# Attention and mixture-of-experts kernel: the loads of the last batch's first pair of heads move in front of the second block's first kept stores

## The chip, the cores and the metric

The kernel runs on 1 core of one Trainium2 chip. Its time is the device time of one execution in microseconds (us), and the number that counts is the median over runs. TensorE is called PE here (PEld is its weight load), VectorE is DVE, ScalarE is ACT, GpSimd is POOL and SyncE is SP. SP does no arithmetic: it issues nearly all loads and stores, one after the other, in the order in which they stand in its queue.

## The reference

The kernel computes two layers one after the other. The first is a linear attention over 4 batches, 8 heads, 576 positions and 64 features a head, with 128 random features; the second is a mixture of 4 experts over all 2304 rows, where every expert is applied to every row and the results are weighted.

```python
def phi(x):                                   # x: (4, 8, 576, 64), omega: (128, 64)
    h = einsum('bhsd,md->bhsm', x, omega) - sum(x * x, -1) / 2
    return exp(h - max(h, -1)) / sqrt(128)
q_p, k_p = phi(q * scale), phi(k * scale)
kv, z = einsum('bhsm,bhsd->bhmd', k_p, v), sum(k_p, axis=2)
x = einsum('bhsm,bhmd->bhsd', q_p, kv) / (einsum('bhsm,bhm->bhs', q_p, z) + 1e-6)
x = x.transpose(0, 2, 1, 3).reshape(2304, 512)
p = probs / (probs.sum(-1) + 1e-9)            # (2304, 4)
out = sum over e of p[:, e] * (maximum(x @ w1[e], 0) @ w2[e])   # w1: (4, 512, 1024), w2: (4, 1024, 512)
```

## The kernel before

**Tiling.** Heads are worked on in pairs, 4 pairs a batch. The 2304 rows of the second layer are cut into blocks: rows 0 to 511 (block 0), rows 512 to 1279 (block 1, 6 tiles of 128) and rows 1280 to 2303 (block 2, 8 tiles). The hidden layer is cut into 8 pieces (expert and half of its 1024 columns), and one piece on one block is a *visit*. Block 1 has 8 visits and block 2 has 8. Each fp32 product is made of three products of rounded halves, so each weight matrix is split into a high part (`w1ah`, `w1sh`, `w2h`, by ACT) and a low part (`w1al`, `w1sl`, `w2l`, by POOL, line 567).

**A visit of block 1** (`fast`). The first matrix product is done in seven partial products with summed operands (`p1` to `p7`, line 934) for each of two groups, and gives the hidden tiles `hh` (ACT, lines 958 and 992) and `hl` (DVE, lines 964 and 995). The second product (`outputs`, lines 753 to 755) runs over six row tiles; three of them are begun early between the partial products. After the last partial product PE needs `hh` and `hl` of line 992 and 995 for the fourth weight chunk of the first row tile. Results are gathered into `acc`.

**Kept weights.** The summed and split first weights that a visit of block 1 makes are stored to memory for block 2: `keep_sides`, line 670, 8 stores a visit, named `kept`. They stand on SP's queue. The next visit's weights go to the same two buffers: the split into `w1ah` (line 564, called as the first step of `sides(v + 1)`) rewrites a buffer which the first store, `kept<-w1ah`, still reads, so it waits until that store has landed. It stands on ACT's queue after `p6(1)`, in front of the three `hh` of `p7(1)`, `p3(1)` and `p4(1)`:

```python
        p3(0)
        if u == 1:
            keep_sides(v)
        p4(0)
        ...
        p6(1)
        if v + 1 != DEEP[0]:
            next(ready, None)      # the split into w1ah
        begun(0)
        p7(1)
```

**The order of the work around it** is written out by hand. The attention of the last batch (4 pairs, `Halves`) is cut into steps, *ticks*, that are run between the pieces of block 1: `opening` is 6 ticks for the first pair (load k, load q, load v and the tails, square k, square q, sum of squares of k), `later_ticks` is 12 ticks a pair and ends with 48. `emit` lets 54 ticks run in the first 80% of the block. A visit has 7 shares: one after the partial products and one after each row tile. Loads go through `Halves.load` (line 247: kd, kn, qd, qn), `load_v` (line 128) and `load_tails` (lines 132 and 133). Between them, SP also issues the raw weights `w1r` and `w2r` (line 549). Every load on SP goes round eight semaphores, and an issue also waits for the landing of the issue eight before it.

Of the kernel before, what the change touches and what calls it, by code (L numbers as in the profile page):

```python
# [14 lines left out]
def attention_moe(ctx, tc, kT, qT, kd, qd, kn, qn, vn, omT, probs, w1, w2, out):  # L15
# [11 lines left out]
    _, NP, D, _ = kT.shape  # L27
# [3 lines left out]
    E, FP, P, _ = w1.shape  # L31
# [18 lines left out]
    def place(hp):  # L50
        return hp % 2 * 2 + hp // 2
# [17 lines left out]
    def f32(ap):  # L69
        return ap.bitcast(F32)  # L70
# [30 lines left out]
    NV = len(HALVES)  # L101
# [136 lines left out]
    class Halves(Pair):  # L238
# [131 lines left out]
        def times(self, part):  # L370
            nu, dn, n = self.num.pop(part)
            for o, c, m in in_ring(self.b * S + 2 * P * part, n):
                nc.gpsimd.tensor_tensor(raw_x[:, place(self.hp), c:c + m], nu[:, o:o + m], dn[:, o:o + m], ALU.mult)

    def opening(p, both=False):

        p.load("k")
        yield
        p.load("q")
        yield  # L380
        p.load_v()
        p.load_tails()
        yield
        p.square("k")
        yield
        p.square("q")
        yield
        p.lengths("k")
        if both:
            p.lengths("q")  # L390
        yield
# [74 lines left out]
    def later_ticks(pairs):  # L466

        for p, then in zip(pairs, pairs[1:] + [None]):
            p.project("k")
            p.project_tails("k")  # L470
            p.maxima("k")
            p.maxima_tails("k")
            p.bias("k")
            yield
            p.exp_tails("k")
            p.exp("k", 0)
            p.lengths("q")
            yield
            p.exp("k", 1)
            yield  # L480
            p.project("q")
            p.project_tails("q")
            p.maxima("q")
            p.maxima_tails("q")
            p.bias("q")
            yield
            p.exp_tails("q")
            p.exp("q", 0)
            if then:
                then.load("k")  # L490
            yield
            p.exp("q", 1)
            if then:
                then.load("q")
            yield
            p.sum_keys()
            if then:
                then.load_v()
                then.square("k")
            yield  # L500
            p.turn(0)
            yield
            p.turn(1)
            if then:
                then.square("q")
            yield
            p.numerators(0)
            if then:
                then.lengths("k")
            yield  # L510
            p.invert(0)
            p.times(0)
            p.numerators(1)
            yield
            p.invert(1)
            p.times(1)
            yield
# [4 lines left out]
    BIG = {1: (START, 6 * P), 2: (START + 6 * P, 8 * P)}  # L522
# [5 lines left out]
    N0 = len(visits)  # L528
# [134 lines left out]
    def keep_sides(v):  # L663

        for i in range(2):
            kept[visits[v][1:3], i] = ts_ = tuple(
                scratch.tile([P, w * H], F32, tag=f"s{visits[v][1:3]}{i}{x}{w}", name="kept", bufs=1) for w in (3, 4) for x in "hl"
            )
            for k, t in zip(ts_, made.pop((v, i))):
                nc.sync.dma_start(k, f32(t))  # L670
# [127 lines left out]
    def store(keep):  # L798
        while len(stores) > keep:
            i, t = stores.pop(0)  # L800
            nc.sync.dma_start(out[i * P:(i + 1) * P], t)
# [90 lines left out]
    def fast(v):  # L892
# [96 lines left out]
        def p4(g):  # L989
            product(g, 4, "u", start=False)  # L990
            ha, hc = (x[:, :n] for x in hs[2 * g + 1])
            nc.scalar.activation(ha, P_[g]["u"], AF.Relu)
            if deep and g == 0:
                nc.scalar.activation(r11[:, 1], P_[0]["u"], AF.Relu)
            nc.vector.scalar_tensor_tensor(hc, P_[g]["u"], 0.0, f32(ha), ALU.max, ALU.subtract)  # L995

        def p3(g):
            product(g, 3, "b5", start=False)
            both(g, 0, 1, "b5", "u2")
# [131 lines left out]
                start_sides2(v + 1)  # L1131
        p3(0)
        if u == 1:
            keep_sides(v)
        p4(0)
        if deep:
# [179 lines left out]
    def first_visit(g1):  # L1316
        hs = [relu(ps, 2 * P) for ps in g1[:2]]
        yield 0.5
        for ps in g1[2:]:
            split_w(lo=nc.vector)  # L1320
            hs.append(relu(ps, 2 * P))
            yield 0.5
        split_w(lo=nc.vector)
        split_w(lo=nc.vector)
        yield 0.5
        for t in range(2):
            ps = bank("g2")
            outputs(0, hs, ps, t, range(FH))
            gather(0, ps, t)
            gathered(0, t)  # L1330
            split_w()
            split_w(lo=nc.vector)
            yield 1

    def first_rest(pairs, then):

        def ahead(hp):
            if hp < NP:
                pairs[hp].project("q", 1)
                pairs[hp].project("q", 2)  # L1340

        def exps(hp):
            if hp < NP:
                pairs[hp].exp("q", 1)
                pairs[hp].exp("q", 2)

        ahead(0)
        pairs[2].square("q1", nc.gpsimd)
        yield
        exps(0)  # L1350
        ahead(1)
        pairs[3].square("q1", nc.gpsimd)
        yield
        for hp, p in enumerate(pairs):
            if hp:
                pairs[hp - 1].finish(1)
            p.turn(1, nc.vector)
            p.turn(2, nc.vector)
            if hp == 0:
                nc.vector.tensor_scalar(om_r, om_r, QS, None, ALU.mult)  # L1360
            if hp:
                next(then, None)
            yield
            exps(hp + 1)
            ahead(hp + 2)
            if hp:
                next(then, None)
            yield
            p.numerators(1)
            yield  # L1370
        pairs[-1].finish(1)
        yield

    def chain(*many):
        for x in many:
            yield from x
# [3 lines left out]
    def emit():  # L1380
        pairs, g1 = begin()
        later = [Halves(b, hp) for b in range(1, B) for hp in range(NP)]
        windows = {
            0: (first_rest(pairs, opening(later[0], both=True)), 15 / 11),
            3: (joint_ticks(later[:-NP]), 76 / 45.4),
            N0: (chain(opening(later[-NP]), later_ticks(later[-NP:])), 54 / (NV * (BIG[1][1] // P + 1) * 0.8)),
        }
        ticks, n, done, per = iter(()), 0, 0.0, 0
        for v in range(len(visits)):
            if v in windows:  # L1390
                for _ in ticks:
                    pass
                ticks, per = windows[v]
                n, done = 0, 0.0
            for share in first_visit(g1) if v == 0 else fast(v) if v >= N0 else plain(v):
                done += share
                while n < done * per:
                    next(ticks, None)
                    n += 1
        store(0)  # L1400
# [61 lines left out]
```

## Time and profile before

| | us |
|---|---|
| median of 3 runs | 885.14 |
| lowest and highest run | 884.5, 887.36 |
| the profiled execution's own time | 884.03 |
| its span, first to last instruction | 882.3 |
| PE busy | 876.0 (99%) |
| DVE busy | 575.6 (65%) |
| POOL busy | 555.9 (63%) |
| ACT busy | 467.9 (53%) |

Durations come from the one profiled execution, whose span is 1.73 us shorter than its own time. A busy PE is not the same as PE at its peak: matmuls overlap, so the distance from one start to the next is what one costs. Block 1 runs from 284.75 us of the span to 566.6 us, and the first visit of it to 317.6 us.

### The profile page before, as it was taken

The numbers are of one execution on the slowest core, as the hardware profiler recorded it, in microseconds if no ns is written. First come the engines' busy times: TensorE is split into PE (matmuls) and PEld (weight loads), VectorE is DVE, ScalarE is ACT, GpSimd is POOL, SyncE is SP. The second block draws the span as 40 slices with busy tenths as digits, with TensorE's granted clock in tenths as the row PEclk, the third lists the DMA queues.
The fourth block names the chain that finished last, engine by engine and source line by source line (L and its number), as shares of the span: only waits on it lengthen the run. The fifth ranks groups of instructions, "written<-read, shape, count | busy, mean of one in ns | idle before, by whom it ended". The sixth has DMA issues, their size and how long they took to land.

```text
span 882.3 us, 14767 instructions
## 1 busy us (share of the span) xinstructions
PE 876.0 (99%) x5484; PEld 787.8 (89%) x5484; DVE 575.6 (65%) x1025; ACT 467.9 (53%) x1039; POOL 555.9 (63%) x494
## 2 busy tenths in 40 slices
PE   9999999999999999999999999999999999999998
PEld 9988888989888998989889899899989898998988
DVE  6765566766667647576766656975748476574847
ACT  6554677676784565546545554544443434444342
POOL 6656455555644554444445346779898887979874
PEclk9999999999999999999999999999999999999999
DMA  7665355444522757536274355645152442425132
GB/s 184 170 225 155 111 162 173 132 138 138 179 67 60 265 163 259 196 132 240 78 275 169 118 215 183 214 154 158 57 179 82 138 163 85 156 60 180 52 117 96
DMA packets 64296, 134.01 MB, mean 152 GB/s; under 512 B 10368, under 2 KB 20800, under 8 KB 64224
## 3 DMA queue, kind: packets, MB, share of 16 engines
q1 hardware_dynamic: 54256, 102.95, 35.8%
q0 software_dynamic: 9360, 29.82, 10.5%
q8 instruction: 43, 0.70, 0.3%
q10 hardware_dynamic: 608, 0.30, 0.1%
q14 instruction: 29, 0.24, 0.1%
HBM read 98.96 MB, written 34.08 MB: 151 GB/s over the span
## 4 chain that ended last, share of the span: by engine, by line
PE 91%; DVE 3%; POOL 2%; DMA 2%; issue 1%; ACT 1%; SPq 0%; POOLq 0%; ACTq 0%; DVEq 0%
PE g L934 28%; PE g L1012 18%; PE g L753 8%; PE g L755 8%; PE g L754 8%; PE g L738 3%; PE g L739 3%; PE g L740 3%; PE kv L317 2%; PE q_ps L266 1%; PE k_ps L266 1%; PE qt_ps L328 1%; DMA kept<-w1ah 1%; PE kv L177 1%; PE nd L358 1%
## 5 line engine op out<-in xcount | busy, mean ns | idle before, releaser
L782 DVE SCALAR_TENSOR_TENSOR acc<-g,pr,acc 128x256 f32<-128x256 f32 (+1 forms) x278 | 140.4, 543 | 41.2 <-PE g L755 25.7
L567 POOL TENSOR_TENSOR w2l<-w2r,w2h 128x512 fp32r<-128x512 f32 x61 | 79.4, 1309 | 77.4 <-ACT w2h L564 65.3
L567 POOL TENSOR_TENSOR w1sl<-w1r,w1sh 128x512 fp32r<-128x512 f32 (+1 forms) x43 | 75.2, 1751 | 65.2 <-ACT w1sh L564 54.5
L753 PE MATMUL g<-w2h,hh 128*128 128x512 f32 x280 | 112.0, 400 | 0.3 <-ACT kp L299 0.2
L755 PE MATMUL g<-w2h,hl 128*128 128x512 f32 x280 | 109.7, 392 | 0.0
L754 PE MATMUL g<-w2l,hh 128*128 128x512 f32 x280 | 109.5, 391 | 0.0
L934 PE MATMUL g<-xbh,w1sh 128*128 128x384 f32 (+1 forms) x256 | 93.0, 363 | 0.0
L934 PE MATMUL g<-xbl,w1sh 128*128 128x384 f32 (+1 forms) x256 | 92.9, 363 | 0.0
L934 PE MATMUL g<-xbh,w1sl 128*128 128x384 f32 (+1 forms) x256 | 92.6, 362 | 0.0
L940 ACT ACTIVATE sum<-g 128x384 f32<-128x384 f32 (+1 forms) x96 | 52.2, 543 | 69.7 <-PE g L934 68.8
L567 POOL TENSOR_TENSOR w1al<-w1r,w1ah 128x512 fp32r<-128x512 f32 (+1 forms) x45 | 51.5, 1160 | 50.9 <-ACT w1ah L564 32.9
L934 PE MATMUL g<-xbh,w1ah 128*128 128x384 f32 (+1 forms) x192 | 69.9, 364 | 0.0
L934 PE MATMUL g<-xbl,w1ah 128*128 128x384 f32 (+1 forms) x192 | 69.6, 362 | 0.0
L934 PE MATMUL g<-xbh,w1al 128*128 128x384 f32 (+1 forms) x192 | 69.5, 362 | 0.0
L948 DVE TENSOR_TENSOR sum<-g,sum 128x384 f32<-128x384 f32 (+1 forms) x64 | 37.4, 587 | 39.6 <-PE g L934 33.6
L755 PEld LDWEIGHTS g<-w2h,hl 128*128 128x128 f32 x280 | 52.5, 188 | 11.8 <-DVE hl L995 0.4
L753 PEld LDWEIGHTS g<-w2h,hh 128*128 128x128 f32 x280 | 52.7, 188 | 10.9 <-DVE sum L948 0.6
L754 PEld LDWEIGHTS g<-w2l,hh 128*128 128x128 f32 x280 | 52.6, 188 | 9.0
L964 DVE SCALAR_TENSOR_TENSOR hl<-sum,hh 128x384 fp32r<-128x384 f32 x48 | 33.2, 695 | 42.0 <-ACT hh L958 41.3
L934 PEld LDWEIGHTS g<-xbh,w1sh 128*128 128x128 f32 x256 | 48.1, 188 | 5.7 <-DVE sum L948 0.6
L934 PEld LDWEIGHTS g<-xbl,w1sh 128*128 128x128 f32 x256 | 48.1, 188 | 5.2
L934 PEld LDWEIGHTS g<-xbh,w1sl 128*128 128x128 f32 x256 | 48.1, 188 | 5.1
(220 smaller groups left out, 2470.1 us busy)
## 6 DMA issues: line engine op xcount, KB each, us to landing
w1r<-in_w SPq DMA_DIRECT2D x54, 512.0 KB, 3.6
w2r<-in_w SPq DMA_DIRECT2D x76, 256.0 KB, 2.9
kept<-w1sh SPq DMA_DIRECT2D x16, 512.0 KB, 5.0
kept<-w1sl SPq DMA_DIRECT2D x16, 512.0 KB, 5.5
w1sh<-kept POOLq DMA_DIRECT2D x16, 512.0 KB, 5.1
w1sl<-kept POOLq DMA_DIRECT2D x16, 512.0 KB, 5.8
kept<-w1ah SPq DMA_DIRECT2D x16, 384.0 KB, 4.3
kept<-w1al SPq DMA_DIRECT2D x16, 384.0 KB, 4.9
```

Source lines behind the costliest of these rows:

```text
L567: lo.tensor_tensor(c, t, f32(a), ALU.subtract)
L738: nc.tensor.matmul(ps[:, :n], a[:, w], hi, start=(hp == 0), stop=False)
L739: nc.tensor.matmul(ps[:, :n], a[:, w], lo, start=False, stop=False)
L753: nc.tensor.matmul(ps, ha[:, ts_], wa, start=(c == 0), stop=False)
L754: nc.tensor.matmul(ps, ha[:, ts_], wc, start=False, stop=False)
L755: nc.tensor.matmul(ps, hc[:, ts_], wa, start=False, stop=(c == FH - 1))
L782: nc.vector.scalar_tensor_tensor(to, ps, sc, to, ALU.mult, ALU.add)
L934: nc.tensor.matmul(ps, a[:, w], x[:, k], start=(start and k + at == 0), stop=(k == 1 and at == 2), skip_group_check=not start)
L940: nc.scalar.activation(t, P_[g][where], AF.Copy)
L948: nc.vector.tensor_tensor(t, P_[g][where], kept, ALU.add)
L964: nc.vector.scalar_tensor_tensor(x, y, 0.0, f32(z), ALU.max, ALU.subtract)
L1012: nc.tensor.matmul(to, x, w, start=(start and f + k == 0), stop=(f + k == 3), skip_group_check=not start)
```

## The change

The loads of the first pair of the last batch leave the ticks and are issued in `fast`, right before `keep_sides` of block 1's first visit. `opening` keeps three ticks for that pair, and 51 ticks run in the same 80% of the block, so that each of them stands at another place than before, the first ones most.

```diff
+    ahead = []
+
     def opening(p, both=False):
 
-        p.load("k")
-        yield
-        p.load("q")
-        yield
-        p.load_v()
-        p.load_tails()
-        yield
+        if both:
+            p.load("k")
+            yield
+            p.load("q")
+            yield
+            p.load_v()
+            p.load_tails()
+            yield
         p.square("k")
...
         if u == 1:
+            for p in ahead:
+                p.load("k")
+                p.load("q")
+                p.load_v()
+                p.load_tails()
+            ahead.clear()
             keep_sides(v)
...
-            N0: (chain(opening(later[-NP]), later_ticks(later[-NP:])), 54 / (NV * (BIG[1][1] // P + 1) * 0.8)),
+            N0: (chain(opening(later[-NP]), later_ticks(later[-NP:])), 51 / (NV * (BIG[1][1] // P + 1) * 0.8)),
...
+        ahead.append(later[-NP])
```

SP's queue in block 1's first visit, before (k and q are inputs of the pair, va and vb its values, kept the stores, w1r and w2r raw weights):

```order
L549 DMA w2r<-in_w 128x512 x3
L670 DMA kept<-w1ah 128x768
L670 DMA kept<-w1al 128x768
...
L670 DMA kept<-w1sl 128x1024
L549 DMA w2r<-in_w 128x512
L247 DMA k<-in_kd 128x576
...
L133 DMA vb<-in_vn 64x4x64
L549 DMA w1r<-in_w 128x1024 x2
```

The same stretch of SP's queue now (line numbers are three higher behind the diff's first new lines):

```order
L552 DMA w2r<-in_w 128x512 x3
L247 DMA k<-in_kd 128x576
L247 DMA k<-in_kn 128x576
L247 DMA q<-in_qd 128x576
L247 DMA q<-in_qn 128x576
L128 DMA va<-in_vn 128x4x128
L132 DMA vb<-in_vn 64x4x64
L133 DMA vb<-in_vn 64x4x64
L673 DMA kept<-w1ah 128x768
L673 DMA kept<-w1al 128x768
...
L552 DMA w2r<-in_w 128x512
```

Seven loads have moved past eight stores and one weight load; nothing was added to the queue or taken from it.

ACT's queue in the same visit now; before, the same operations stand in the same order, and the first row waits for the same store, under the name of another semaphore:

```order
L567 ACTIVATE w1ah<-w1r 128x512 [waits DMAHW2_49,Pool_49]
L567 ACTIVATE w1ah<-w1r 128x256
L961 ACTIVATE hh<-sum 128x384 [waits DVE_49] x2
L995 ACTIVATE hh<-g_3654 128x384 [waits PE_49]
L783 ACTIVATE acc<-g_3762,pr 128x512 [waits PE_49]
```

The split that waits for the first kept store still stands in front of the last hidden tiles of the visit.

PE's queue, the key projections of the pair (k_ps, t_ps) between the row tiles of the first visit (g_3851 is the fourth tile), before:

```order
L753 MATMUL g_3851<-w2h,hh 128x512
L754 MATMUL g_3851<-w2l,hh 128x512
L755 MATMUL g_3851<-w2h,hl 128x512
L266 MATMUL k_ps<-om_r,k 128x128 x8
L277 MATMUL t_ps<-om_r,k 128x128 x2
L753 MATMUL g_3894<-w2h,hh 128x512
```

And now, where the rows in front of them belong to the second row tile (g_3778):

```order
L756 MATMUL g_3778<-w2h,hh 128x512
L757 MATMUL g_3778<-w2l,hh 128x512
L758 MATMUL g_3778<-w2h,hl 128x512
L266 MATMUL k_ps<-om_r,k 128x128 x8
L277 MATMUL t_ps<-om_r,k 128x128 x2
L756 MATMUL g_3802<-w2h,hh 128x512
```

The projections have moved from behind the fourth row tile to behind the second.

## Rows read from the trace of the kernel before

**Rows 1.** The page, section 1: busy us, share of the span, instructions.

```profile
PE 876.0 (99%) x5484; PEld 787.8 (89%) x5484; DVE 575.6 (65%) x1025; ACT 467.9 (53%) x1039; POOL 555.9 (63%) x494
```

**Rows 2.** Waits of PE, whole span: who waited for whom, us, times, longest.

```profile
PE g L753 <- ACT kp L299: 0.2, 1, 0.2
```

**Rows 3.** Waits of ACT in block 1, same columns.

```profile
ACT w1ah L564 <- DMA kept<-w1ah: 16.8, 9, 3.1
```

**Rows 4.** Timeline of ACT, first visit: start us, us, instruction [idle before, releaser].

```profile
300.33 0.94 ACT L564 ACTIVATE w1ah<-w1r 128x512 fp32r<-128x512 f32 x2 [3.06 <-DMA kept<-w1ah]
...
302.78 0.53 ACT L958 ACTIVATE hh<-sum 128x384 fp32r<-128x384 f32 x1 [1.09 <-DVE sum L948]
303.21 0.47 ACT L992 ACTIVATE hh<-g 128x384 fp32r<-128x384 f32 x1
```

**Rows 5.** Timeline of DVE, same stretch.

```profile
301.71 0.56 DVE L964 SCALAR_TENSOR_TENSOR hl<-sum,hh 128x384 fp32r<-128x384 f32 x1 [2.29 <-ACT hh L958]
...
304.20 0.55 DVE L995 SCALAR_TENSOR_TENSOR hl<-g,hh 128x384 fp32r<-128x384 f32 x1
```

**Rows 6.** Timeline of PE, same stretch.

```profile
304.22 0.39 PE L753 MATMUL g<-w2h,hh 128*128 128x512 f32 x1
304.45 0.39 PE L754 MATMUL g<-w2l,hh 128*128 128x512 f32 x1
304.80 0.50 PE L755 MATMUL g<-w2h,hl 128*128 128x512 f32 x1
```

**Rows 7.** Timeline of SP, first visit of block 1 (issues only).

```profile
296.72 0.42 SPq L670 DMA_DIRECT2D kept<-w1ah  x1
...
304.56 1.13 SPq L549 DMA_DIRECT2D w2r<-in_w  x1
305.79 1.09 SPq L247 DMA_DIRECT2D k<-in_kd  x1
...
309.57 0.60 SPq L133 DMA_DIRECT2D vb<-in_vn  x1
```

**Rows 8.** The store issued at 296.72 alone: issue to landing.

```profile
DMA to landing us min/median/max: 3.5/3.5/3.5
```

**Rows 9.** The weight load issued at 304.56 alone: issue to landing.

```profile
DMA to landing us min/median/max: 5.3/5.3/5.3
```

**Rows 10.** Both vb loads, issued at 308.97 and 309.57: issue to landing.

```profile
DMA to landing us min/median/max: 4.7/4.9/5.1
```

**Rows 11.** Timeline of SP in block 0, another batch's first pair: four loads, then three.

```profile
53.22 0.42 SPq L247 DMA_DIRECT2D k<-in_kd  x1
...
54.64 0.43 SPq L247 DMA_DIRECT2D q<-in_qn  x1
...
61.49 0.38 SPq L128 DMA_DIRECT2D va<-in_vn  x1
...
62.57 0.60 SPq L133 DMA_DIRECT2D vb<-in_vn  x1
```

**Rows 12.** The q load issued at 54.64 alone: issue to landing.

```profile
DMA to landing us min/median/max: 5.5/5.5/5.5
```

**Rows 13.** Instructions on tile k issued 305.7 to 307.4: who waited for them, us, times.

```profile
  POOL k L251: 2.4, 1
```

**Rows 14.** The chain of waits, pieces of 66 partial-product matmuls: start us, us, what.

```profile
466.66 11.94 PE g L934 x66
503.14 11.44 PE g L934 x66
```

**Rows 15.** Timeline of PE: the first matmuls of the span, and the longest stop.

```profile
1.06 3.77 PE L1188 MATMUL warm<-om_r 128*128 128x128 f32 x16 [1.06 <-DVE om_r L1179]
4.90 2.25 PE L147 MATMUL k_ps<-om,k 128*128 128x128 f32 x18
...
126.79 0.94 PE L266 MATMUL q_ps<-om_r,q 64*128 64x128 f32 x12 [1.12 <-DVE qtl L339]
```

**Rows 16.** Spans and mean granted TensorE clock of the core.

```profile
core 0: 882.3 us, clock 1.000
```

## The prediction

> **What bounds the kernel now.** The page's first section comes first: PE is busy 876.0 of the 882.3 us of the span, the other engines 53 to 65% [rows 1]. The list of PE's waits comes next, because a busy PE may still be late: behind block 0 it holds one wait, of 0.2 us [rows 2]. So PE's queue sets the end, block 2 included, and a stop of PE in block 1 is not caught up by anything that waits now: it moves the end by its own length. The question is then only where the change makes PE stop, or spares it a stop.
>
> The third view is the list of ACT's waits in block 1. ACT waits for the store `kept<-w1ah` nine times, 16.8 us in total and 3.1 at most [rows 3]. The longest one is in the first visit, just where the change puts seven loads in front of that store. The timelines of ACT, DVE and PE there show how close this wait is to PE. ACT stands still for 3.06 us, splits w1ah from 300.33 us on, and only then makes the last hidden tiles, the one of line 992 at 303.21 [rows 4]. DVE's first low part there had itself waited 2.29 us for ACT, and its last one runs from 304.20 to 304.75 [rows 5]. PE starts the matmul that reads this tile at 304.80, while its two neighbours are 0.23 us apart and it could have started at 304.68 [rows 6]. PE already waits here, for 0.12 us: the chain store, ACT, DVE, PE has no slack left, and what is added to the landing of the store is added to PE.
>
> **The change part by part.**
>
> *The store is issued later.* SP issued it at 296.72 us [rows 7], and it landed 3.5 us later [rows 8], at 300.22, 0.11 us ahead of the split that waits for it [rows 4]. Nothing is waited for by the seven loads that now stand in front of it, since their tiles were last used before block 1's first visit. So they go out from 296.72 on. What they cost the store can be read in three ways.
> - From below, by SP's issue alone. In block 0 the four loads take from 53.22 to 55.07 (54.64 + 0.43), and the three from 61.49 to 63.17 [rows 11]: 1.85 + 1.68 = 3.5, and a handover of 0.05 between them makes 3.6 us. If the store then lands 3.5 us after its issue as before, it is 3.6 us late.
> - By their data, when the queue is full. The weight load in front of the same seven loads was issued at 304.56 and landed 5.3 us later [rows 7, 9], at 309.86; the last of the seven, issued at 309.57, landed 4.7 us later [rows 7, 10], at 314.27. The seven take 4.4 us of the DMA engines.
> - From above, by the slowest such loads. In block 0 the last of four loads landed 5.5 us after its issue at 54.64 [rows 11, 12], which is 6.9 us after the first was issued at 53.22; the three others with their 1.68 us and the store itself, a quarter of the seven's bytes and so some 1.1 us, behind that make 9.7 us after 296.72, or 306.4: 6.2 us late.
>
> I take 4.4 us, because it is of the same seven loads on a busy queue, with a weight load in flight in front of them, as it will be at the new place. The range of this term is 3.6 to 6.2.
>
> *What is queued behind it.* ACT is in order: both splits, then the hidden tiles of line 958 and line 992, then a gather. The whole chain of rows 4 and 5 moves by 4.4 us: the hidden tile of line 992 ends at 303.68 + 4.4 = 308.1, and the low part at 304.75 + 4.4 = 309.15. PE has work up to 304.22, stops for 3.9 us until about 308.1, runs two matmuls, and stops again until 309.2, where it was at 304.80. PE is 4.4 us late. POOL's part of the split waits for the second store and moves as well, and so do the next weight loads; all of these are needed only in the second visit, by a PE that is itself 4.4 us later. They cost nothing more.
>
> *What is gained at the same place.* The pair's keys are in memory earlier. Only POOL waited for them, 2.4 us [rows 13], while PE ran row tiles; PE itself had no wait there [rows 2]. So an end to POOL's wait is worth nothing at the end of the kernel. The key projections go from behind the fourth row tile to behind the second; that is still behind PE's own stop, when the keys, in front of the store on the queue, have long landed.
>
> *The ticks move.* 54 ticks in 44.8 shares become 51: the first tick of the pair's projections falls on the third share instead of the fifth, and the shift shrinks to none at the end of the 80%. PE has the same matmuls. What can change is how PE's small waits fall. A stretch of 66 partial-product matmuls takes 11.44 us undisturbed and 11.94 where projections stand right ahead of it [rows 14], so the placement is worth 0.5 us a visit. With six visits that hold attention the sum could be anything from 3.0 us less to, if every one of them got such a place, 3.0 us more; since one such stretch was there before and one stands at the end of the second visit now, I take nothing. Exponentials and the keeps of ACT keep their order around the start of each visit, with the same number of operations, so I see no new wait as long as the first one.
>
> The sum: 884.03 + 4.4 = 888.4 us for an execution like the profiled one. That execution is 1.1 us under the median of 885.14, so as a median I predict 885.14 + 4.4 = 889.5 us.
>
> **The rivals.**
>
> *PE's clock falls in the stop.* PE ran at a mean granted clock of 1.000, its level of 2.4 GHz, over the whole span [rows 16], and stopped 1.12 us at most in it, with no sign in the matmuls behind [rows 15]. A stop of 3.9 us is in no row. The nearest rows are the first of the span: 16 matmuls of 128 columns took 3.77 us, 0.24 each, and the 18 behind them 2.25 us, 0.125 each [rows 15], so PE works at about half pace until it has worked for 3.8 us. Half pace for as long again would cost 3.77 - 16 x 0.125 = 1.8 us, together 6.2, and a time of 891.3. The Trainium skill (TensorE: Matmul & The Clock Gate, "What's actually happening") says that an idle PE goes back to 1.2 GHz and that activity lifts it again; by that rule this rival is the likelier the longer the stop, and no run here shows it yet.
>
> *PE catches up in the ticks.* This is the case that ends on the other side, not slower. The places of the projections decide 0.5 us in each of six visits [rows 14]; if all six came out well, 3.0 of the 4.4 us come back: 886.5 us. It decides from 1.8 us on, since 4.4 - 1.8 is 2.6 and no longer to be told from nothing. For it speaks that the pair's work starts earlier; against it that the chain shows only one stretch of 11.94 and PE's own waits hold only 0.2 us [rows 2], so there is little to win back.
>
> *The store is not what holds ACT, so that the change does nothing.* A wait is put down to the last of several semaphores, and POOL's earlier split is another one here. Then only the 0.2 us [rows 2] could go: 884.9. Against it: the landing at 300.22 and the start at 300.33 fit [rows 4, 8], and nine waits of this kind are in the list [rows 3].
>
> **How the numbers follow.** Late by the store alone, 3.6 to 6.2 us: 0.68. With the clock: 0.15. Caught up in the ticks: 0.10. No effect of the store: 0.07, half of it a small gain. 0.3% is 2.7 us and about what can be told from no change here; a 0.02 of the first case falls under it, when the low end meets a median at the low end of the three runs. So slower: 0.66 + 0.15 = 0.81; the same: 0.02 + 0.10 + 0.03 = 0.15; faster: 0.04. The range leaves out the clock's upper tail and the two cases without a loss at its lower end: 886.8 (3.6 less half of what the ticks could return, 1.5, and a low median) to 892.5 (the clock case with a somewhat slower store).
>
> **What would show it.** Right: in the first visit SP issues the store near 300.3, ACT's wait for it is about 7.5 us instead of 3.06, PE has a stop of some 3.9 us near 304.3 and all later visits start about 4.4 us later. The clock's rival would show as a granted clock under 1.0 behind the stop. Wrong would be an ACT wait that is as short as before, a PE that runs through, or visits whose lateness shrinks from one to the next.

## The result, and the profile after

The changed kernel took 895.1 us (median of 6 runs, 894.85 to 896.27), the kernel before beside it 885.85 (6 runs, 883.28 to 887.36): a ratio of 1.0107, 95% interval 1.0083 to 1.0131. So it is slower, by some 9.3 us where 4.4 were predicted, and outside the range. The profiled execution has a span of 893.2 us at a mean clock of 0.994 (before: 882.3 and 1.000 [rows 16]); the terms below are of these two, 10.9 us apart. Lines behind the added code have moved by 3: L937 is line 934 of before, L943 is 940, L961 is 958, L967 is 964, L995 is 992, L998 is 995, L567 is 564, L756 to L758 are 753 to 755.

The first section of the page shows that PE has the same 5484 matmuls and is busy 3.8 us longer [rows 1], so most of the loss is standing still, and part of it is slower matmuls:

```profile
PE 879.8 (98%) x5484; PEld 790.2 (88%) x5484; DVE 580.6 (65%) x1025; ACT 468.1 (52%) x1039; POOL 556.2 (62%) x494
```

The list of PE's waits (who waited for whom, us, times, longest) had one line of 0.2 us in the second block [rows 2]. Now it has two stops, one behind ACT's last hidden tile and one behind ACT's keep of a sum (a keep copies a partial product into `sum`, line 943):

```profile
PE g L756 <- ACT hh L995: 5.8, 1, 5.8
PE g L937 <- ACT sum L943: 1.8, 1, 1.8
PE q_ps L266 <- ACT kp L306: 0.4, 1, 0.4
```

**The first stop** is in block 1's first visit, where it was expected. ACT's waits in block 1, same columns, have their longest at 8.7 us instead of 3.1 [rows 3]:

```profile
ACT w1ah L567 <- DMA kept<-w1ah: 21.7, 7, 8.7
```

In SP's timeline (start, us, issue) the loads go out from 295.82 on and the store at 300.60; before, it went out right behind the weight load [rows 7]:

```profile
295.40 0.33 SPq L552 DMA_DIRECT2D w2r<-in_w  x1
295.82 0.38 SPq L247 DMA_DIRECT2D k<-in_kd  x1
...
299.96 0.60 SPq L133 DMA_DIRECT2D vb<-in_vn  x1
300.60 0.60 SPq L673 DMA_DIRECT2D kept<-w1ah  x1
```

The store alone, from issue to landing, answering to [rows 8]:

```profile
DMA to landing us min/median/max: 4.3/4.3/4.3
```

So it lands at 304.9. ACT's timeline [rows 4] starts there, and its last hidden tile is at 308.70:

```profile
305.02 0.93 ACT L567 ACTIVATE w1ah<-w1r 128x512 fp32r<-128x512 f32 x2 [8.69 <-DMA kept<-w1ah]
...
308.27 0.52 ACT L961 ACTIVATE hh<-sum 128x384 fp32r<-128x384 f32 x1 [1.90 <-DVE sum L951]
308.70 0.47 ACT L995 ACTIVATE hh<-g 128x384 fp32r<-128x384 f32 x1
```

Behind the landing the chain is longer than before. From the landing to the matmul that reads the last low part PE needs (`hl` of L998) it takes 5.45 us (304.94 to 310.39), before 4.58 (300.22 to 304.80 [rows 6]). DVE's first low part took 1.37 us instead of 0.56 [rows 5], beside POOL's low part of the split. That split began 1.15 us behind the landing of the first store. In the kernel before it waited for the second store and began 2.34 us behind the landing of the first:

```profile
306.40 1.37 DVE L967 SCALAR_TENSOR_TENSOR hl<-sum,hh 128x384 fp32r<-128x384 f32 x1 [7.91 <-ACT hh L961]
...
309.79 0.55 DVE L998 SCALAR_TENSOR_TENSOR hl<-g,hh 128x384 fp32r<-128x384 f32 x1
```

```profile
306.09 2.27 POOL L570 TENSOR_TENSOR w1al<-w1r,w1ah 128x512 fp32r<-128x512 f32 x2 [8.72 <-ACT w1ah L567]
```

The same POOL operation before:

```profile
302.56 2.31 POOL L567 TENSOR_TENSOR w1al<-w1r,w1ah 128x512 fp32r<-128x512 f32 x2 [4.25 <-DMA kept<-w1al]
```

PE's timeline [rows 6] stops behind 303.06. Behind the stop the matmuls that were 0.23 us apart are 0.58 to 0.60 apart, while `hl` of L998 is ready only at 310.34, then 0.42, up to 312.3:

```profile
303.06 0.40 PE L758 MATMUL g<-w2h,hl 128*128 128x512 f32 x1
309.22 0.80 PE L756 MATMUL g<-w2h,hh 128*128 128x512 f32 x1 [5.77 <-ACT hh L995]
...
310.39 0.79 PE L758 MATMUL g<-w2h,hl 128*128 128x512 f32 x1
...
311.41 0.63 PE L757 MATMUL g<-w2l,hh 128*128 128x512 f32 x1
311.84 0.63 PE L758 MATMUL g<-w2h,hl 128*128 128x512 f32 x1
...
312.62 0.40 PE L757 MATMUL g<-w2l,hh 128*128 128x512 f32 x1
312.85 0.39 PE L758 MATMUL g<-w2h,hl 128*128 128x512 f32 x1
```

The table by stretches (us, then PE, PEld, DVE, ACT, POOL busy, granted clock, DMA share, GB/s) shows the clock beside it: it fell to its lower level, 1.2 GHz, while PE stood still and stayed there for the first matmuls behind. Work at this level is called half pace below:

```profile
303.00:305.50 2.50, 0.45 (x2) 0.01 (x1) 0.00 (x0) 0.48 (x1) 0.00 (x0) 1.00 1.04 415
305.50:309.20 3.70, 0.00 (x0) 0.00 (x0) 2.21 (x3) 1.77 (x5) 3.11 (x3) 0.53 1.02 412
309.20:312.50 3.30, 3.28 (x7) 2.22 (x8) 3.20 (x7) 1.27 (x3) 1.68 (x2) 0.50 0.92 344
312.50:316.00 3.50, 3.50 (x30) 2.71 (x30) 1.82 (x5) 0.93 (x2) 2.03 (x2) 1.00 0.02 7
```

**The second stop** was not expected. It is at the start of the fifth visit, 436.37 us. In ACT's timeline six exponentials of q stand in front of the visit's first keep `sum`; in the kernel before four exponentials of k stood there, which waited for nothing, and q's came behind the keeps:

```profile
439.20 0.74 ACT L306 ACTIVATE qp<-t_ps,nbq 64x128 f32<-64x128 f32 x2 [2.79 <-DVE nbq L293]
439.95 1.14 ACT L299 ACTIVATE qp<-q_ps,nbq 128x128 f32<-128x128 f32 x4
440.97 0.51 ACT L943 ACTIVATE sum<-g 128x384 f32<-128x384 f32 x1
```

The same place before:

```profile
427.74 1.13 ACT L299 ACTIVATE kp<-k_ps,nbk 128x128 f32<-128x128 f32 x4
429.93 0.49 ACT L940 ACTIVATE sum<-g 128x384 f32<-128x384 f32 x1 [1.05 <-PE g L934]
```

The exponentials of q wait for DVE's bound `nbq`. DVE's line 292, an operation on 9 columns, took 1.23 us, while POOL's split of w1sl ran (436.49 to 438.88); its row of before, at 430.42, says 0.17:

```profile
437.04 0.60 DVE L287 TENSOR_REDUCE mxq<-t_ps 64x1 f32<-64x128 f32 x2
437.67 1.23 DVE L292 SCALAR_TENSOR_TENSOR mxq<-sqq,mxq 128x9 f32<-128x9 f32 x1
438.94 0.17 DVE L293 SCALAR_TENSOR_TENSOR nbq<-sqq,mxq 128x9 f32<-128x9 f32 x1
```

PE waits for the keep until 441.53, and behind this short stop the clock fell again:

```profile
441.53 0.45 PE L937 MATMUL g<-xbh,w1sh 128*128 128x384 f32 x1 [1.85 <-ACT sum L943]
```

```profile
442.20:445.60 3.40, 3.40 (x12) 3.40 (x11) 0.00 (x0) 1.48 (x4) 2.39 (x2) 0.50 0.56 205
445.60:449.00 3.40, 3.40 (x21) 3.40 (x21) 2.31 (x5) 1.96 (x5) 0.00 (x0) 1.00 0.35 77
```

**Where the time went.** A visit's length is taken from its first matmul (in PE's timeline) to that of the next. Within a visit, each matmul's distance to the next above the median of its kind gives what was lost.
- The first visit is 41.85 us instead of 32.83. Of the 9.0 more, 1.3 are q's projections, which came over from a later visit; 5.8 is the stop, 1.8 was lost at half pace behind it. Not all of the 1.8 is the clock's price: part of it is the wait for `hl` of L998, and experiment 5, where the clock stayed up, puts the clock at 1.0.
- The fifth visit is 41.02 us instead of 38.03, 3.0 more: the stop lost 2.0 us and the half pace 1.6, and 0.6 of smaller waits of before are gone.
- The other visits of block 1 are 0.1 us shorter together, in spite of the 1.3 us of projections that left them.
- Block 1 starts at 283.83 us instead of 284.75, 0.9 earlier, before any changed instruction; from block 2 on all visits have the same lengths to 0.02 us.

Together 9.0 + 3.0 - 0.1 - 0.9 = 11.0, of the 10.9 between the spans.

### The profile page after: what moved, and what is told of

Same layout as the page of the kernel before. It is cut to its first block, busy times and chain, and to the rows that moved or that the text cites. A ratio compares the mean times of both kernels' runs of the same rounds, so it can differ in the third digit from the quotient of the medians.

```text
span 893.2 us, 14771 instructions
## 1 busy us (share of the span) xinstructions
PE 879.8 (98%) x5484; PEld 790.2 (88%) x5484; DVE 580.6 (65%) x1025; ACT 468.1 (52%) x1039; POOL 556.2 (62%) x494
## 4 chain that ended last, share of the span: by engine, by line
PE 92%; DVE 3%; DMA 1%; POOL 1%; issue 1%; ACT 1%; SPq 0%; POOLq 0%; ACTq 0%
PE g L937 30%; PE g L1015 18%; PE g L756 8%; PE g L758 8%; PE g L757 8%; PE g L741 3%; PE g L742 3%; PE g L743 3%; PE kv L317 2%; PE k_ps L266 1%; PE q_ps L266 1%; PE qt_ps L328 1%; PE kv L177 1%; PE nd L207 1%; PE nd L358 1%
## 5 line engine op out<-in xcount | busy, mean ns | idle before, releaser
L756 PE MATMUL g<-w2h,hh 128*128 128x512 f32 x280 | 112.7, 403 | 6.0 <-ACT hh L995 5.8
L758 PE MATMUL g<-w2h,hl 128*128 128x512 f32 x280 | 110.2, 394 | 0.0
L937 PE MATMUL g<-xbh,w1sh 128*128 128x384 f32 (+1 forms) x256 | 93.3, 364 | 1.8 <-ACT sum L943 1.8
L937 PE MATMUL g<-xbl,w1sh 128*128 128x384 f32 (+1 forms) x256 | 93.1, 363 | 0.0
L937 PE MATMUL g<-xbh,w1sl 128*128 128x384 f32 (+1 forms) x256 | 92.8, 362 | 0.0
L943 ACT ACTIVATE sum<-g 128x384 f32<-128x384 f32 (+1 forms) x96 | 52.2, 543 | 76.5 <-PE g L937 75.6
L937 PE MATMUL g<-xbh,w1ah 128*128 128x384 f32 (+1 forms) x192 | 70.5, 367 | 0.0
L937 PE MATMUL g<-xbl,w1ah 128*128 128x384 f32 (+1 forms) x192 | 70.1, 365 | 0.0
L937 PE MATMUL g<-xbh,w1al 128*128 128x384 f32 (+1 forms) x192 | 69.9, 364 | 0.0
L756 PEld LDWEIGHTS g<-w2h,hh 128*128 128x128 f32 x280 | 53.0, 189 | 17.2 <-ACT hh L995 6.2
L967 DVE SCALAR_TENSOR_TENSOR hl<-sum,hh 128x384 fp32r<-128x384 f32 x48 | 34.5, 723 | 49.6 <-ACT hh L961 48.9
L758 PEld LDWEIGHTS g<-w2h,hl 128*128 128x128 f32 x280 | 52.8, 188 | 12.1 <-DVE hl L998 0.7
L937 PEld LDWEIGHTS g<-xbh,w1sh 128*128 128x128 f32 x256 | 48.1, 188 | 8.0 <-ACT sum L943 2.2
L937 PEld LDWEIGHTS g<-xbl,w1sh 128*128 128x128 f32 x256 | 48.2, 188 | 5.2
L937 PEld LDWEIGHTS g<-xbh,w1sl 128*128 128x128 f32 x256 | 48.2, 188 | 5.1
```

The lines of the kernel that those rows point to most:

```text
L756: nc.tensor.matmul(ps, ha[:, ts_], wa, start=(c == 0), stop=False)
L758: nc.tensor.matmul(ps, hc[:, ts_], wa, start=False, stop=(c == FH - 1))
L937: nc.tensor.matmul(ps, a[:, w], x[:, k], start=(start and k + at == 0), stop=(k == 1 and at == 2), skip_group_check=not start)
L943: nc.scalar.activation(t, P_[g][where], AF.Copy)
L967: nc.vector.scalar_tensor_tensor(x, y, 0.0, f32(z), ALU.max, ALU.subtract)
```

## The experiments

Theory A: the loads cost what they delay the first kept store, and the three ticks less cost something of their own. Its rivals changed as results came in. All medians stand beside runs of the kernel before on the same chip. "Block 2" and "second block" in some of the texts quoted below are block 1 of the text above, its first visit the one at 284 us.

**1. Loads alone.** The loads in front of the stores, and the old 54 ticks:

```diff
+        else:
+            yield
+            yield
+            yield
         p.square("k")
-... later_ticks(later[-NP:])), 51 / ...
+... later_ticks(later[-NP:])), 54 / ...
```

> The seven loads stand in front of the first kept stores, but the 54 ticks stay where they were (three empty ticks stand for the moved loads). Theory A, two separate losses (the store is late, so ACT, so PE stops and then runs at half pace, about 7.6 us; the moved ticks cost about 4 us in the fifth visit): PE stops some 5.9 us at the fourth chunk of the first row tile, the granted clock falls behind it, no stop in the fifth visit, and about 7 us over before. Rival B, the whole loss hangs on the moved ticks: as before within 2 us. Rival C, the late store brings the second stop about as well: about 10 us over before, with both stops.

894.34 us, ratio 1.0099 (1.0081 to 1.0116). PE's waits in block 1:

```profile
PE g L760 <- ACT hh L999: 5.6, 1, 5.6
PE g L760 <- DVE sum L955: 1.2, 1, 1.2
```

The first visit is 8.5 us longer: 5.8 of stop and 3.0 of half pace, less 0.2 of small waits of before. The fifth visit is as before (37.95 us): the second stop isn't the loads'. A new one of 1.2 us is in the sixth visit (last section).

**2. Ticks alone.** 51 ticks, the loads right behind the stores:

```diff
-            for p in ahead: ...   # the loads
-            ahead.clear()
             keep_sides(v)
+            for p in ahead: ...
+            ahead.clear()
```

> 51 ticks at their new places, but the seven loads right behind the eight kept stores of the first visit. Theory A: no stop of PE in the first visit over 0.3 us, a stop of about 2 us at the partial products of the fifth visit with a lower granted clock behind it, 3 to 4 us over before. Rival B: 9 us over before. Rival C: as before within 1.5 us, since nothing is late any more.

893.25 us, ratio 1.0089 (1.0069 to 1.0108), twice what was expected. It wasn't the ticks alone: the projections of k now came before k had landed, behind eight stores, and that is a stop of its own, with the clock low behind it. The fifth visit has the second stop, though no load stands in front of a store:

```profile
PE k_ps L266 <- DMA k<-in_kd: 3.3, 1, 3.3
PE g L937 <- ACT sum L943: 1.8, 1, 1.8
```

**3. Split later.** The changed kernel, but in the first visit ACT's splits into w1ah stand behind the last hidden tiles:

```diff
-        if v + 1 != DEEP[0]:
+        if v + 1 != DEEP[0] and v != N0:
             next(ready, None)
...
         p4(1)
+        if v == N0:
+            next(ready, None)
```

> The changed kernel, but in the first visit of block 1 the split into w1ah stands on ACT behind the last hidden tiles instead of in front of them. Theory A (ACT's wait for the store holds up the hidden tiles behind it): the store lands as late as in the changed kernel, near 305 us, ACT waits for it, and PE has no stop in the first visit; about 7 us under the changed kernel, with the stop of the fifth visit left. Rival: the loads slow PE or the stores by their traffic, not through ACT's queue: within 2 us of the changed kernel.

892.23 us, ratio 1.0072 (1.0052 to 1.0093): 2.9 us back, not 7. In the profiled executions the first visit is 1.7 us shorter than in the changed kernel, and the fifth 1.6, where the clock stayed up behind the same stop. The stop at 309 is gone, so it was that order on ACT; but POOL's squares, which stand behind its part of the splits, come late, with them the maxima and the exponentials, and PE stops at 319 us instead:

```profile
PE t_ps L277 <- ACT kp L306: 3.1, 1, 3.1
PE g L937 <- ACT sum L943: 1.8, 1, 1.8
```

**4. Loads early.** 51 ticks, the loads at the start of the first visit:

```diff
+        for p in ahead: ...   # the loads
+        ahead.clear()
         p1(0)
         prepare()
```

> 51 ticks at their new places, and the seven loads at the very start of block 1's first visit, in front of the partial products and of the last weight loads that SP waits for, some 10 us ahead of the kept stores. Theory A: the kept store lands about as early as before, no stop over 0.5 us in the first visit, the stop of the fifth visit is left: 3 to 4 us over before, as with the ticks alone. Rival: loads at any place of this visit ahead of the stores cost PE their stop: 7 us or more over before.

891.33 us, ratio 1.0063 (1.0044 to 1.0083). There the loads stand in front of three weight loads, and what was the store's wait becomes the weights': ACT waits for w2r, and PE at 300.7 us for the keep behind it (3.5 us of the 5.4).

```profile
299.65 0.63 ACT L567 ACTIVATE w2h<-w2r 128x512 fp32r<-128x512 f32 x1 [3.85 <-DMA w2r<-in_w]
```

**5. Keep PE busy.** 18 spare matmuls in front of the tile where PE stood still, overwritten by the real ones:

```diff
-        begun(2)
+        if v == N0:
+            ...   # the third tile's first six matmuls, three times
+            outputs(v, hs, g2[2], 2, range(2))
+        else:
+            begun(2)
```

> The changed kernel with 18 spare matmuls (128x512, at 0.227 us each some 4.1 us) that compute the third output tile's first sums three more times over, and are overwritten, right in front of the third output tile of block 2's first visit, where TensorE stood still for 5.8 us. Theory (the clock has a price of its own): TensorE is busy during most of the wait, so its clock stays at 1.0 there, and the 2.1 us lost at half pace behind the stop are won back: 892.5 to 894, some 2 us under the changed kernel's 895.1. Rival (the half pace hid behind later waits, or the spare work pushes the rest back): 895 to 898, with the stop shorter by as much as the spare work takes and the clock still falling, or no gain though it doesn't fall.

894.45 us, ratio 1.0095 (1.0062 to 1.0129). The profiled run is the 892.99 one: the clock was 1.000 over the whole span, the stop fell to 1.7 us and 4.1 us of spare work stood in its place, so the same wait cost no half pace. The first visit is 40.88 us, 1.0 less than in the changed kernel with the store as late (21.1 us behind the visit's start in both). The other 0.8 of the 1.8 would have been a wait anyway, for the last low part: in both traces 1.17 us lie between the first matmul behind the stop and the one that reads it (309.22 to 310.39, and here 309.88 to 311.05):

```profile
311.05 0.50 PE L758 MATMUL g<-w2h,hl 128*128 128x512 f32 x1 [0.44 <-DVE hl L998]
```

So the theory's 2.1 us were too many, and the rival's "hid behind later waits" was right in part. The median of the five lies between the two ranges. The time goes with the clock: 892.99 us at a mean clock of 1.000, 893.99 and 894.45 at 0.998, 895.77 and 895.84 at 0.996. That is 2.8 us from the first to the last, with the same program.

**6. Two of the seven loads.** Old ticks; k's two loads in front of the stores, five behind:

```diff
+            for p in ahead:
+                p.load("k")
             keep_sides(v)
+            for p in ahead: ...   # q, v and the tails
```

> Old 54 ticks; of the seven loads only the two of k stand in front of the kept stores, the five of q and v behind them. Theory (the stop in the first visit is as long as the first store is late): the store is issued some 1 us later instead of 4.8 us, so TensorE stops for 1.0 to 1.8 us instead of 5.65 us; if the clock stays up 1 to 2 us over the kernel before, if it falls 2.5 to 3.5 us over it; 887 to 889.5. Rival (any load beside the stores slows their flight, whatever its place): as with all seven in front, 892 to 895.

890.97 us, ratio 1.0057 (1.0036 to 1.0078), between the theory's range and the rival's: 3.2 us of stop where 1.0 to 1.8 were expected, so theory A in its form "as late as the issue" is wrong. SP issued the store only 1.0 us later, but it landed 5.7 us behind its issue instead of 3.5 [rows 8]. The second line is a stop in the sixth visit (last section):

```profile
PE g L760 <- ACT hh L999: 3.2, 1, 3.2
PE g L760 <- DVE sum L955: 2.0, 1, 2.0
```

**7. Hold one tick.** The changed kernel, with q's exponentials at the end of the fourth visit put off behind the fifth's partial products:

```diff
-                while n < done * per:
+                held_back = v == N0 + 3 and done > 27.5
+                while n < done * per and not held_back:
```

> The changed kernel, with the tick of q's exponentials at the end of the fourth visit of the second block put off into the fifth, behind its partial products, so that those exponentials don't stand on ScalarE in front of the fifth visit's keep. Theory (the second loss is this tick's place alone): the stop of 1.85 us at the fifth visit's start and the half pace behind it go, and the time falls by 3 to 4 us to 891 to 892.5. Rival (it is late because the first visit's stop has pushed the chain of exponentials back, or another wait takes its place): 894 to 896, with a stop of 1.5 us or more elsewhere in the fifth or sixth visit.

895.01 us, ratio 1.0095 (1.0063 to 1.0126): nothing gained in the median. The stop of 1.85 us went, as theory says, and the clock didn't fall there; but smaller waits took its place, the longest of them 0.9 us for q's features (`qtl`), and the fifth visit is 39.66 us, 1.6 above before. That is 1.4 less than in the changed kernel. In the profiled execution it is lost again: block 1 starts 0.8 us later, and the first visit is 0.6 longer, with a shorter stop and more half pace behind it. PE's two longest waits:

```profile
PE g L756 <- ACT hh L995: 5.3, 1, 5.3
PE nd L358 <- DVE qtl L339: 0.9, 1, 0.9
```

**8. The control.** Old ticks with three empty ones, all seven loads right behind the stores (the edits of 1 and 2 together).

> The control: old 54 ticks (three of them empty), and the seven loads in one bunch right behind the eight kept stores. Theory (only the place in front of the stores and the three ticks cost something): the time of the kernel before, 885 to 887, with no stop of TensorE over 0.5 us in the second block. Rival (the bunch of seven loads itself is what costs, by its traffic beside the stores and the visit's weight loads): 889 to 892.

884.8 us, ratio 0.9994 (0.9973 to 1.0015); the only wait in block 1 is the old one. So the bunch of loads costs nothing by itself.

```profile
PE g L760 <- ACT kp L299: 0.2, 1, 0.2
```

**9 and 10. A packet of code.** Between the landings of k's two loads of the changed kernel lie 2.5 us, and between those of the first two stores of before 2.2; a packet of instructions moves on the DMA engines each time. Five more spare matmuls at the start of the kernel before, eleven more at that of the changed one, pull it ahead:

```diff
-        for i in range(8):
+        for i in range(13):    # 9; 19 in 10
             nc.tensor.matmul(warm[:, :P], om_r, om_r, start=True, stop=True)
```

> The kernel before with 13 instead of 8 spare matmuls at its very start (some 1 us more there). TensorE's code is loaded in packets of 16 KB on the same DMA engines; in the kernel before one lies at 299.68 us, 2.96 us behind the issue of block 2's first kept store, and the store after that one lands 2.2 us behind it. More instructions ahead pull this packet some 2 us earlier, to the time of the first store's issue. Theory (the packet holds up whatever lands next, and a store behind it pays 1.5 to 2 us): the first store lands 5 to 5.5 us behind its issue instead of 3.5, TensorE stops 1.3 to 2 us in the first visit; 887 to 889.5. Rival (the packet is harmless; the hole behind it has another cause): flight 3.5 us as before, no stop, 886 to 887.

> The changed kernel with 19 instead of 8 spare matmuls at its start (some 2 us more there): the packet of TensorE's code at 298.36 us, in the middle of the seven loads, moves in front of the first of them. Theory: the hole of 2.5 us between the landings of k's two loads goes, the first kept store lands 1 to 1.7 us sooner than in the changed kernel, the stop of 5.8 us falls to 4.1 to 4.8 us; by the start's 2 us the total stays at 894 to 897. Rival: the hole stays where it is between those two loads and the stop at 5.5 to 6 us.

Experiment 9: 884.75 us, ratio 0.9996 (0.9984 to 1.0007). The packet came 4.5 us earlier in the visit, further than meant, and was over before the weight load and the stores were issued, so no stop came; the hole between the stores went with it, and the second landed 3.8 us behind its issue instead of 5.2. Experiment 10: 897.03 us, ratio 1.0134 (1.0109 to 1.0158), stop 5.6 us. The packet left, the hole between k's loads shrank to 1.0 us, and one of 1.9 appeared between q's; the store landed 21.0 us behind the visit's start, as in the changed kernel (21.1). The packet didn't set the first stop.

**11. Another queue.** Old ticks; ACT issues the loads, in front of its w1ah split:

```diff
+        for p in ahead if v == N0 else ():
+            p.load("k", eng=nc.scalar)
+            ...   # q, v, tails
         if v + 1 != DEEP[0]:
             next(ready, None)
```

> Old 54 ticks; the seven loads are issued by ScalarE on its own DMA queue, right in front of its w1ah split, in the time in which it waits for the first kept store, and no longer by SyncE in front of the stores. Theory A (what costs is the loads' place in front of the stores in one queue): the first store is issued as in the kernel before and lands up to 1.5 us later, TensorE stops 0 to 1.5 us; 885 to 888. Rival B (what costs is 1.5 MB of loads on the same DMA engines at that time, whatever the queue): the store lands 3 us or more later, the stop is 3 to 5 us, 890 to 894.

891.6 us, ratio 1.0073 (1.0052 to 1.0094); a stop of 5.2 us. The store landed only 1.2 us later than before behind the visit's start, but ACT couldn't use it: its own issues had to wait for earlier transfers on their semaphores, the last until 305.4, and the split stands behind them. So the time fits rival B and the cause doesn't; whether a queue that no engine waits behind would be free of cost stays open.

```profile
302.43 0.70 ACTq L132 DMA_DIRECT2D vb<-in_vn  x1
305.37 0.55 ACTq L133 DMA_DIRECT2D vb<-in_vn  x1
306.02 0.94 ACT L571 ACTIVATE w1ah<-w1r 128x512 fp32r<-128x512 f32 x2 [8.46 <-DMA q<-in_qn]
```

**12. Loads in front, split later, old ticks** (the edits of 1 and 3).

> Old 54 ticks, the seven loads in front of the kept stores as in the changed kernel, and in block 2's first visit ScalarE's w1ah splits, the ones that wait for the first kept store, put behind its parts of the last hidden tiles. Theory (the loads' price comes in only by that wait in front of the hidden tiles; with later ticks nothing else is short): no stop over 0.5 us near 304 to 320 us, the clock stays up, 885 to 887.5, the kernel before's time. Rival (what is held up just comes later: the splits of the next weights and the squares behind them on GpSimd are 5.6 us late and TensorE stops for them further on, as it did for 3.1 us with 51 ticks): 888 to 892.

893.26 us, ratio 1.009 (1.0074 to 1.0107): the rival, and above its range (the profiled execution is the slowest of four, 896.51). There is no stop near 309, but one of 5.9 us at 320 to 326, at the second visit's first keep. It stands on ACT behind ten exponentials of k. Their bound stands on DVE behind four sums of the next weights (L691 to L694), and these wait for POOL's part of the delayed splits until 312.7. Then they take 5.6 us instead of 1.8, beside POOL's work. POOL's square of k was ready at 313.8 and was not what they waited for. The second line is a stop in the sixth visit again.

```profile
PE g L941 <- ACT sum L947: 5.9, 1, 5.9
PE g L760 <- DVE sum L955: 2.6, 1, 2.6
```

No version beats the kernel before; 8 and 9 equal it.

**The store's landing sets the first stop.** Landings are issue plus issue-to-landing, in us:

| kernel | last load ahead lands, behind the weight load in front of it | store lands, behind the visit's start | PE's stop |
|---|---|---|---|
| before | - | 15.5 | 0.1 |
| 8 (none ahead) | - | 15.6 | none |
| 6 (k alone) | 3.5 | 18.6 | 3.2 |
| 7 | 5.6 | 20.7 | 5.3 |
| changed | 6.0 | 21.1 | 5.8 |
| 1 | 6.0 | 21.0 | 5.6 |
| 10 | 6.0 | 21.0 | 5.6 |

The stop is as long as the store is late against the kernel before, to 0.2 us. In the seven kernels that have all seven loads in front (changed, 1, 3, 5, 7, 10 and 12) these land 5.6 to 6.4 us behind the weight load, although SP issues them in 3.6 to 4.8.

## Why the prediction was wrong

- *What bounds the kernel*: right. All that PE lost in block 1 is at the end of the span.
- *The store lands later, and ACT, DVE and PE with it*: the mechanism was right (experiments 3, 6 and 8), and the size was off: 4.4 us was taken, from the same loads at another place in the queue, and 5.6 came (15.5 to 21.1), inside the term's 3.6 to 6.2. "The seven take 4.4 us of the DMA engines" is the figure that failed: here they took 6.0. Where they stand elsewhere on SP's queue (before and experiments 2, 4, 8 and 9) they took 4.4 to 4.9, behind a transfer that had itself flown 4.1 to 5.7 us from issue to landing; in the seven kernels with all of them in front they took 5.6 to 6.4, behind a weight load that had flown 2.6 to 2.7. The difference is mostly one gap between two landings, 1.9 to 2.5 us in the seven and 1.0 to 1.5 in the others. What makes it is open; experiment 10 shows that the packet of code alone doesn't.
- *"They cost nothing more"*: wrong for POOL's part of the split. It did not move with the chain but came closer to the landing, and DVE's low parts beside it made the chain 0.9 us longer. No term of the sum stood for that.
- *The clock's rival* had 0.15 and happened. It was priced at 1.8 us. Behind the first stop 1.8 were lost at half pace (3.0 in experiment 1), but experiment 5 shows that 1.0 of them were the clock's, so that the price fits is in part luck. "Until it has worked for 3.8 us" did not hold behind a stop: PE worked at half pace for 3.3 us behind the changed kernel's first stop (309.2 to 312.5) and for 6.2 in experiment 1 (310.5 to 316.7). The clock fell behind the second stop as well, which the rival did not have. The row of the 1.12 us stop without a sign [rows 15] was taken for comfort. The Trainium skill's rule (TensorE: Matmul & The Clock Gate, "What's actually happening"), that an idle PE goes back to 1.2 GHz, held for the first stop: the granted clock was 0.53 over its second part.
- *"The ticks move": nothing* was the step that failed outright. "Exponentials and the keeps of ACT keep their order around the start of each visit" was not so: at the fifth visit ACT got q's exponentials in front of the keep instead of k's. That term was to be between -3.0 and +3.0, by projections on PE alone; that it came to the end of this range is luck, for the cause is another. The stop stands in all six kernels with 51 ticks in their places (changed and 2, 3, 4, 5 and 10) and in none of the seven with 54, whose fifth visits take 37.8 to 38.0 us. It cost 3.0 us in the fifth visit: about 1.4 us by the wait, as experiments 3 (39.46 us) and 5 (39.43) show, in which the same stop stood and the clock stayed up; and 1.6 by the clock, as the 41.0 us of the changed kernel and of experiment 2 show.
- *"PE catches up in the ticks"* and *"the change does nothing"*: wrong. The third visit got 0.9 us shorter, but all visits of block 1 other than the first and the fifth only 0.1 together; and the store does hold ACT.
- *Late splits cost nothing in the second visit*: right while PE was as late as they were. Experiments 3 and 12 show what is under it: with PE kept on time, the delayed splits stop it for 3.1 us in the first visit and for 5.9 in the second.

By the two traces the sum should have read, in the prediction's own terms: 5.6 for the store (4.4 was taken), 0.9 for DVE beside POOL's split, 1.0 for the clock behind the first stop and 3.0 for the ticks in the fifth visit (nothing was taken for these three), 10.5 in all. With what moved between the visits and the earlier start (1.3 - 0.1 - 0.9) that makes 10.8 of the 10.9 us between the spans.

## What to carry to other kernels

Price a transfer that is put ahead in a queue by the landing of the last one, on a queue as full as it will be there, and not by the time that the issues take; the same seven loads took 4.4 to 6.4 us here, by their place. When the steps of a side job shift against the main loop, read the new order of the in-order engine that serves both at each loop's start, above all where its inputs are made late. The lower clock behind a stop of PE cost 1.0 us and 1.6 us here, so put it into the sum, and not only into a rival; but take off what PE would have waited there anyway.

## What the runs showed of the hardware

- The fifth visit's stop was followed by the lower clock in three kernels (changed, 2 and 10) and the same stop at the same place in three others (3, 4 and 5) was not; it was 1.80 to 1.85 us in the first three and 1.84 to 1.85 in the others. So whether a short stop costs the clock isn't settled by its length alone.
- A packet of PE's code can hold back a store. The kernel's 43 packets of 16 KB fit 10,968 instructions of PE and PEld at 255 each. In the sixth visit it lay in front of the stores in the kernel before and in experiment 8, and the first store landed 3.4 to 3.5 us behind its issue. In experiments 1, 6 and 12 it came 2.4 to 2.8 us later in the visit, among the stores; it took 1.6, 2.3 and 2.6 us, the store 4.7, 5.5 and 6.1, and PE stopped for 1.2, 2.0 and 2.6. Of the 84 first stores of the visits 2 to 7 in the fourteen kernels these three alone took longer than 3.8 us, and in these three alone the packet began within 2 us behind the issue. Experiment 9 moved a packet away from the second store of the first visit, and that store landed 3.8 us behind its issue instead of 5.2. The packet's line in experiment 6, from 481.3 to 486.3 us (packets, MB, share of 16 engines; one engine's 2.3 us), and the store's:

```profile
q8 instruction: 1, 0.02, 2.9%
```

```profile
DMA to landing us min/median/max: 5.5/5.5/5.5
```

  Why it came later there is open. The Trainium skill (Runtime: NRT & Kernel Launch, "Instruction fetch mechanics") says that code comes in blocks of 16 KiB, 256 instructions, and that a block's cost is mostly hidden; the size agrees, and in these three kernels the cost was not hidden.
- A short operation of DVE took several times as long beside a long one of POOL. Of DVE's operations on 9 columns with two input tiles, the 589 in the fourteen traces that ran with none of POOL's two-tile operations (`TENSOR_TENSOR`) beside them took 0.17 us each; the 78 that lay almost wholly beside one took 1.20 in the median and up to 1.90. For those that make the low parts of hidden tiles (384 columns) it is 0.54 to 0.56 us in 572 alone, and 1.33 in the median of 138 beside.
